# Seven block products in place of eight in the out-projection of a sparse-attention and gated-MLP kernel

## The chip, the cores and the metric

The kernel runs on one core of one Trainium2 chip. The time is the device time of one execution in microseconds (us); the median of three runs of the kernel before is 524.06 us (523.08 to 524.91). The profile is of one execution, whose span from the first to the last instruction is 520.8 us.

## The reference

Eight batches, eight heads, 576 positions, head width 64. Four heads of each batch use a local band of 32 keys, four a strided mask; the attention output x of a batch (576 x 512) feeds a gated block:

```
h = np.maximum(x @ w_in, 0.0)                # 512 -> 1024
u, v = h[..., :512], h[..., 512:]
v_n = (v - mean(v)) / np.sqrt(var(v) + 1e-06)
v_s = np.einsum('ts,bsd->btd', w_spatial, v_n) + b_spatial[None, :, None]
gated = u * v_s
return (gated @ w_out).astype(np.float32)    # 512 -> 512
```

Inputs are float32 (the two weight matrices come as 64-bit words). Every matrix factor is split into a rounded high part and the rest, and each product is the sum of three matmuls: high x high, high x rest, rest x high (PROD, L65).

## The kernel before, in words

**Layout.** A batch's x is held as four tiles (one for two heads, 128 rows of the 512 features), each with a high and a rest part, in the ring x (8 buffers). The positions are 576 = 4 x 128 + 64, for outputs with positions along the columns two halves of 288 (HS, called hf). Rings are sets of buffers that are used in turn: a new tile takes the oldest buffer and waits for all users of the tile that held it.

**Stages of one batch.** *V* (first half of moe_1, L891): four 128 x 512 tiles v = relu(x w_in_v), 12 matmuls of 512 columns each, then a chain on ScalarE, VectorE and GpSimd (relu, batch-norm statistics, normalise, split; chain, L828). *U* (second half of moe_1): eight 128 x 288 tiles u = relu(w_in_u^T x^T), 12 matmuls each, into two buffers of the ring u. *Tail* (moe_tail, L949): the last 64 positions of V, for batches 0 and 1 alone, then for two batches in one. *Gate* (spatial in moe_2, L984): per half, four tiles of 14 matmuls (L997, L1009, L1010), each multiplied into u in place by VectorE (L1019) and then split into high and rest in two buffers of the ring g (L372 or L374, and L382). *Out-projection* (project, L1030): per half, four output tiles e; each sums over four feature blocks f and three products, 12 matmuls of 128 x 288 (L1039), in one bank of the ring m (4 banks of PSUM); then one copy to the ring o (2 buffers, L394 or L396) and one store. moe_2 runs gate half 0, out-projection half 0, gate half 1, out-projection half 1. A batch has 96 matmuls of L1039.

**Order.** All instructions are known ahead and the order of each engine's queue is fixed before the run: a planner (Program.order, L173) walks through a list of operations with modelled costs and, on each engine, takes the ready operation with the smallest key. Keys come from the stage's place in the list plan (L1070), for attention from interpolated due times, and for the setup from the table KEYS. Where an operation may go to several engines (a rounding: ScalarE, VectorE, GpSimd; a rest: VectorE, GpSimd), the planner chooses by its own costs. The entries dp and dpt of KEYS bias that choice up to a given time. The plan is V 0, U 0, tail 0, gate and out-projection 0, the same for batch 1, then V 2, U 2, tail of 2 and 3, gate and out-projection 2, V 3, U 3, and so on. Attention units (32, one for two heads; eight of them before V 1 ends) go between them. The kernel puts idle matmuls (L1172) into gaps of PE early on.

**Weights.** w_in comes in eight tiles (u and v, four each), w_out in four, as 64-bit words: ScalarE (L750), GpSimd or VectorE (L758, L755) and VectorE (L766) turn each into float32, then a rounding and a rest (L382) give the two parts. weights() (L776) sorts the twelve jobs by their keys; the first four use the still empty tile vn as their landing place, then jobs take buffers of the rings g and u in turn (odd jobs g, even jobs u). So the first u tiles of batch 0 take the buffers of the last two even jobs: before, the u weights of block 3 and the w_out rows of block 2.

Of the kernel before, what the change touches and what calls it, by code (L numbers as in the profile page):

```python
# [40 lines left out]
    "a": (-825.9, -1662.1, -696.1, -506.6, 76.7, 35.0, 162.7, 122.5,),  # L41
    "v": (-216.6, -1140.4, -156.0, 19.8,),
    "u": (-158.4, -165.3, 0.3, 367.0,),
    "s": (2476.0, -453.8, 2782.5, 3198.4,),
    "t": (2534.3,),
    "o": (641.4, -137.9, 1268.2, 1486.2,),
    "cst": (-2628.8,),
    "lead": (-0.22,),
    "fill": (170.7, 2011.8, -4312.7, 693.0, -265.9, 735.5,),
    "dp": (844, -15182,),  # L50
    "dpt": (83.09,),
    "lv": (-430.1, -2526.4, -200.5, -140.6,),
    "lu": (-99.7, -488.1, -137.6, -250.6,),
    "lo": (435.1, 82.8, -874.1, 81.6,),
    "ls": (781.6, 39.6, 3113.7, 831.6, 1021.7,),
    "near": (122.22,),
# [6 lines left out]
PROD = ((0, 0), (0, 1), (1, 0))  # L63
FLAT = {2: "p n -> p n", 3: "p a b -> p (a b)", 4: "p a b c -> p (a b c)"}
# [244 lines left out]
def pe_cost(m, n):  # L309
    return max(m / 1.2, 4.8 + 0.4464 * n)  # L310
# [3 lines left out]
def attention_moe(ctx, tc, qT, kT, ks, vl, vs, cst, eye, w_in, w_out, wsp, wtail, out):  # L314
# [14 lines left out]
    w_out_sb = sb.tile([P, 2, NT, DM], F32R, name="w_out_sb")  # L329
# [26 lines left out]
    r_o = Ring(sb, "o", [P, HS], F32, 2)  # L356
# [5 lines left out]
    r_pm = Ring(ps, "m", [P, 512], F32, 4)  # L362
# [86 lines left out]
    def local_attention(t, due, q, kl, v, vin, kin):  # L449
# [45 lines left out]
        for u in range(nu):  # L495
# [22 lines left out]
            def f_e(eng, f0=f0, u=u, m=m):  # L518
# [8 lines left out]
                due - 10, [(ACT, (95 if t in APART else 278) + 0.833 * 2 * STRIDE)], f_e,  # L527
# [200 lines left out]
    def weight(key, fetch, src, n, dst, tok, stage):  # L728
# [7 lines left out]
        if src.dtype == F32:  # L736
            val = lambda: buf().bitcast(F32).rearrange(FLAT[len(buf.ring.shape)])[:, 2 * i * n : 2 * i * n + n]
            load(fetch, val, src, [(buf, i, 0), (buf, i, 1)], P * n * 4)
        else:
# [5 lines left out]
            val = lambda dt=F32: half(1, dt)  # L745
            load(fetch, lambda: raw(I32), src.bitcast(I32), [low, top], P * n * 8)
# [25 lines left out]
        lo_in = [(buf, i, 0), (buf, i, 1)] if src.dtype == F32 else [top]  # L772
        rnd(key, n, lambda: dst(0), val, lo_in, [(*tok, 0)])
        rest(key, n, lambda: dst(1), val, lambda: dst(0), lo_in + [(*tok, 0)], [(*tok, 1)])

    def weights():  # L776
        jobs = []
        for i in range(NT):
            rows = slice(i * P, (i + 1) * P)
            for c, name in enumerate("uv"):  # L780
                cols = slice(c * HF, (c + 1) * HF)
                jobs.append((
# [8 lines left out]
        for n, job in enumerate(jobs):  # L791

            def put(job=job, n=n):
                stage = (first, n) if n < NT else ((r_g if n % 2 else r_u).new(), 0)
                weight(*job, stage)
# [459 lines left out]
```

## Time and profile before

| what | value |
|---|---|
| median of three runs | 524.06 us |
| span of the profiled execution (the page gives no other time of it) | 520.8 us |
| difference between the median and that span | 3.3 us |
| TensorE matmul busy | 508.6 us, 98% |
| VectorE busy | 334.5 us, 64% |
| ScalarE busy | 228.4 us, 44% |
| GpSimd busy | 83.0 us, 16% |
| out-projection matmuls (L1039) | 768, 107.3 us |

The share of an engine is an average over the span; the first 70 us and the rest differ, so the table is to be read together with the stretches below. PE stands for TensorE's matmuls, PEld for its weight loads, DVE for VectorE, ACT for ScalarE, POOL for GpSimd and SP for the queue that issues the DMAs.

### The profile page before, as it was taken

What the parts mean: (1) busy time and instruction counts of PE and PEld (TensorE: products, weight loads), DVE (VectorE), ACT (ScalarE), POOL (GpSimd) and SP (SyncE); (2) the same over time, 40 slices, a digit from 0 to 9 for tenths busy, and PEclk for the clock granted to TensorE, in tenths of its full rate; (3) what the DMA queues carried; (4) which work ended last, traced back from release to release, by engine and by line L of the source; (5) the groups of instructions that cost most, each with busy time, mean ns of one, the idle gap of its engine ahead of it and who ended that gap; (6) DMA issues with size and microseconds to landing.
All of it is one profiled execution on the core that took longest, in us unless ns stands there. A gap on an engine that the chain in (4) does not pass through costs nothing.

```text
span 520.8 us, 14553 instructions
## 1 busy us (share of the span) xinstructions
PE 508.6 (98%) x5980; PEld 467.6 (90%) x5980; DVE 334.5 (64%) x1042; ACT 228.4 (44%) x717; POOL 83.0 (16%) x168
## 2 busy tenths in 40 slices
PE   6899999999999999999999999999999999999997
PEld 3579899889998999989999899998999899998997
DVE  4999996696765758658556667748556553427132
ACT  6778855474533654226432355325432242213111
POOL 2453411133011212002020110102101020001000
PEclk9999999999999999999999999999999999999999
DMA  8968553451333223132233212331102200110011
GB/s 282 338 223 273 186 154 118 135 202 31 102 111 133 79 80 110 47 111 79 80 134 105 85 28 75 133 133 55 49 33 64 87 1 1 47 45 1 1 45 47
DMA packets 26242, 52.65 MB, mean 101 GB/s; under 512 B 3136, under 2 KB 11584, under 8 KB 26176
## 3 DMA queue, kind: packets, MB, share of 16 engines
q1 hardware_dynamic: 26176, 51.72, 29.9%
q8 instruction: 47, 0.77, 0.6%
q14 instruction: 19, 0.16, 0.1%
HBM read 42.27 MB, written 9.44 MB: 99 GB/s over the span
## 4 chain that ended last, share of the span: by engine, by line
PE 87%; DVE 6%; ACT 5%; DMA 1%; issue 1%; SPq 0%; POOL 0%; ACTq 0%; DVEq 0%; POOLq 0%
PE m L1039 20%; PE m L997 19%; PE m L916 17%; PE m L874 17%; PE po L677 3%; PE po L574 3%; PE s L464 2%; PE s L607 2%; PE m L1009 2%; PE m L1010 2%; ACT pl L521 1%; DVE w_in_sb L382 1%; DMA vn<-w_in 1%; ACT ptl L372 1%; DVE x L382 0%
## 5 line engine op out<-in xcount | busy, mean ns | idle before, releaser
L997 PE MATMUL m<-wsp_sb,vn 128*128 128x288 f32 x768 | 111.0, 296 | 0.0
L1039 PE MATMUL m<-g,w_out_sb 128*128 128x288 f32 x768 | 107.3, 298 | 0.0
L916 PE MATMUL m<-x,w_in_sb 128*128 128x288 f32 x768 | 106.2, 297 | 0.5 <-DVE w_in_sb L382 0.5
L997 PEld LDWEIGHTS m<-wsp_sb,vn 128*128 128x128 f32 x768 | 105.2, 189 | 0.9
L916 PEld LDWEIGHTS m<-x,w_in_sb 128*128 128x128 f32 x768 | 103.5, 188 | 2.3 <-DVE w_in_sb L382 0.7
L1039 PEld LDWEIGHTS m<-g,w_out_sb 128*128 128x128 f32 x768 | 103.6, 188 | 0.5
L874 PE MATMUL m<-w_in_sb,x 128*128 128x512 f32 (+1 forms) x408 | 100.2, 399 | 0.5 <-DVE x L382 0.4
L874 PEld LDWEIGHTS m<-w_in_sb,x 128*128 128x128 f32 (+1 forms) x408 | 73.8, 185 | 20.3 <-DVE x L382 1.1
L394 ACT COPY o<-m 128x288 f32<-128x288 f32 x61 | 24.3, 398 | 95.3 <-PE m L1039 80.4
L1019 DVE TENSOR_TENSOR u<-m,u 128x288 f32<-128x288 f32 x64 | 28.0, 452 | 43.5 <-PE m L1010 43.4
L850 POOL TENSOR_TENSOR bn<-bn,sel 128x1 f32<-128x1 f32 (+1 forms) x37 | 21.0, 568 | 185.6 <-DVE bn L845 181.8
L374 POOL TENSOR_SCALAR ptl<-pc 32x64 f32<-32x64 f32 (+3 forms) x74 | 28.8, 389 | 124.2 <-PE po L574 71.7
L521 ACT ACTIVATE pl<-pl,ml 128x64 f32<-128x64 f32 (+1 forms) x140 | 47.0, 338 | 1.8 <-DVE ml L501 1.7
L382 DVE TENSOR_TENSOR x<-po,x 128x288 fp32r<-128x288 f32 x64 | 27.3, 447 | 24.9 <-ACT x L394 24.4
L837 DVE BATCH_NORM_STATS2 bn<-vv 128x6 f32<-128x512 f32 (+1 forms) x37 | 25.4, 689 | 27.5 <-ACT vv L832 27.3
L832 ACT ACTIVATE vv<-m 128x512 f32<-128x512 f32 (+1 forms) x37 | 21.8, 595 | 45.9 <-PE m L874 43.7
L930 ACT ACTIVATE u<-m 128x288 f32<-128x288 f32 x64 | 25.8, 407 | 31.1 <-PE m L916 30.9
L394 ACT CAST x<-po 128x288 fp32r<-128x288 f32 x53 | 20.5, 399 | 39.5 <-PE po L574 27.1
L857 DVE TENSOR_SCALAR vv<-vv,bn 128x512 f32<-128x512 f32 (+1 forms) x37 | 20.5, 555 | 16.3 <-POOL bn L850 16.3
L382 DVE TENSOR_TENSOR g<-u,g 128x288 fp32r<-128x288 f32 x64 | 28.7, 464 | 2.0 <-ACT g L372 0.5
L521 ACT ACTIVATION_READ_ACCUMULATOR pl<-pl,ml 128x1 f32 (+1 forms) x140 | 26.6, 190 | 0.0
L501 DVE CUSTOM_DVE_ANT_0 pl<-s,cst_sb 128x64 f32<-128x64 f32 (+1 forms) x140 | 22.5, 214 | 3.0 <-PE s L464 3.0
(119 smaller groups left out, 564.8 us busy)
## 6 DMA issues: line engine op xcount, KB each, us to landing
q<-qT SPq DMA_DIRECT2D x32, 295.0 KB, 4.3
outT<-o SPq DMA_DIRECT2D x64, 144.0 KB, 1.8
v_raw<-vs SPq DMA_DIRECT2D x15, 512.0 KB, 4.0
v_raw<-vl SPq DMA_DIRECT2D x16, 384.0 KB, 3.6
k<-kT SPq DMA_DIRECT2D x16, 304.0 KB, 4.5
kbd<-ks SPq DMA_DIRECT2D x32, 144.0 KB, 3.6
vn<-w_in SPq DMA_DIRECT2D x4, 512.0 KB, 5.5
u<-w_in SPq DMA_DIRECT2D x3, 512.0 KB, 5.8
```

Of the source, the lines that this page charges most:

```text
L374: eng.tensor_scalar(dst(), src(), 1.0, 0.0, op0=ALU.mult, op1=ALU.add)
L382: eng.tensor_tensor(dst(), src(), f32(hi()), op=ALU.subtract)
L394: eng.copy(dst(), src())
L501: eng.tensor_tensor_reduce(out=p_sb()[:m, u, :], in0=s_ps[u % 2]()[:m, f0 : f0 + 2 * STRIDE], in1=msk[:m], scale=-SCALE, scalar=3.0e38, op ...
L521: eng.activation(p_sb()[:m, u, :], src, AF.Exp, bias=st()[:m, u : u + 1], scale=SCALE if masked else -1.0, **total,)
L837: lambda eng: eng.bn_stats(bn()[:m, 0:6], v()[:m]), [(v,)], [(bn,)],
L874: eng.matmul(v_ps()[:m, :], x_at(kt)[:, a, :], w_in_sb[:, w, kt, HF:], start=(n == 0 and i == 0), stop=(n == NT - 1 and i == 2),)
L916: eng.matmul(u_ps()[:, :HS], w_in_sb[:, w, kt, f * P : (f + 1) * P], xs[NHP * b + kt]()[:, a, r], start=(n == 0 and i == 0), stop=(n == NT ...
L930: lambda eng, u=u, f=f, u_ps=u_ps: eng.activation(u()[:, f * HS : (f + 1) * HS], u_ps()[:, :HS], AF.Relu),
L997: eng.matmul(s_ps()[:, :HS], vn()[:, a, kt, fs], wsp_sb[:, w, kt, r], start=(kt == 0 and i == 0), stop=False,)
L1019: lambda eng, ug=ug, s_ps=s_ps: eng.tensor_tensor(ug(), s_ps()[:, :HS], ug(), op=ALU.mult),
L1039: eng.matmul(o_ps()[:, :HS], w_out_sb[:, w, f, e * P : (e + 1) * P], g[a]()[:, f, :], start=(f == 0 and i == 0), stop=(f == NT - 1 and i = ...
```

## The change

The out-projection of a batch is written as a 2 x 2 by 2 x 2 block product (blocks of features x output columns, and features x position halves) with seven products in place of eight. One product is two feature blocks (r) x two output tiles (j) x three matmuls = 12 matmuls, so a batch has 84. The left factors are four blocks (11, 12, 22 and sums s1 to s4) that are made once from w_out: eight subtractions or additions of 256 columns, and 14 blocks of 256 columns are split where eight 512-column halves were. The right factors are blocks of the gated u or differences of them, made in place in u: eight subtractions of 288 columns for each batch; 14 roundings and 14 rests for each batch where there were eight of each. Sums of products stay in PSUM: two banks (xb) are read after product 11, after s2 and after s3, while more products are added to them; six VectorE additions read a bank and add to a kept part.

Gate and out-projection are stages of their own. V of the next batch stands before the out-projection; the out-projection of batch 0 stands after U and tail of batch 1 (U_FIRST), and u of batch 1 lies in the ring x. The ring o has four buffers. The two banks xb are skipped by other users meanwhile, and the ring m is written as four rings of one bank. The rings g and u keep two buffers; the operands of successive products take the two buffers of g in turn. KEYS is replaced; sorted by the new keys the weight jobs are v2, v0, v1, v3, u2, u0, u1, o1 (two tiles), u3, o0 (two tiles), where "o1" and "o0" are the two halves r of w_out.

```
-    w_out_sb = sb.tile([P, 2, NT, DM], F32R, name="w_out_sb")
+    w_out_sb = sb.tile([P, 2, 2, len(BLOCKS), DM // 2], F32R, name="w_out_sb")
-    r_o = Ring(sb, "o", [P, HS], F32, 2)
+    r_o = Ring(sb, "o", [P, HS], F32, 4)
...
+    def combine(key, n, dst, a, b, op, reads, writes):
+        add(
+            key, [(DVE, 70 + 1.04 * n), (POOL, 120 + 2.3 * n)],
+            lambda eng: eng.tensor_tensor(dst(), a(), b(), op=op), reads, writes,
+            port=(DVE, POOL),
+        )
...
+        combine(key, h, left(sa), right(va), right(vb), ALU.add, [ta, tb, la], [("sum", r, 1)])
+        combine(key, h, right(sa), left(va), right(va), ALU.subtract, [ta, la], [("sum", r, 3)])
+        combine(
+            key, h, left(sb_), left(sa), left(va), ALU.subtract, [ta, ("sum", r, 1), lb], [("sum", r, 2)],
+        )
+        combine(
+            key, h, right(sb_), left(vb), left(sb_), ALU.subtract, [tb, ("sum", r, 2), lb],
+            [("sum", r, 4)],
+        )
+        for name, n, val, reads in (
+            ("11", 1, left(va), [ta]), ("12", 2, vb, [tb]), ("s1", 2, sa, [("sum", r, 1), ("sum", r, 3)]),
+            ("s2", 2, sb_, [("sum", r, 2), ("sum", r, 4)]),
+        ):
+            at = BLOCKS[name]
+            split(
...
+            u = us[b, hf] = (r_x if b in U_IN_X else r_u).new()
...
+    def project_out(b, key):
...
+        def operand(key, r, hf, f, slot):
+            g, half = gs[slot], r
+            at = lambda j: g()[:, 2 * half + j]
+            split(
+                key - KEYS["pre"][0], HS, at, (g, half), block(u[hf], f), [(u[hf], f)],
+            )
+            return at, [(g, half, 0), (g, half, 1)]
...
+        def multiply(key, name, src, bank, slot, first=True):
+            for r in range(2):
+                given = operand(key + 0.74 * r, r, *src[r], slot)
+                for j in range(2):
+                    product(key + 0.74 * r + 0.37 * j, name, r, j, bank[j], given, first)
...
+        multiply(key, "11", [(0, 0), (0, 1)], xb, 0)
+        for r in range(2):
+            total(key, (1, r), (0, r), ALU.subtract, (0, r))
+        multiply(key + step, "s1", [(0, 0), (0, 1)], zb, 1)
+        for j in range(2):
+            keep(key + step, o1[j], xb[j], [(o1[j],)])
+        for r in range(2):
+            total(key + step, (1, 2 + r), (0, r), ALU.subtract, (0, r))
+        multiply(key + 2 * step, "s2", [(0, 0), (0, 1)], xb, 0, False)
+        for r in range(2):
+            total(key + 2 * step, (1, 2 + r), (1, r), ALU.subtract, (1, r))
+        for j in range(2):
+            keep(key + 2 * step, o5[j], zb[j], [(o5[j],)])
+        multiply(key + 3 * step, "s4", [(1, 2), (1, 3)], zb, 1, False)
...
+        multiply(key + 4 * step, "s3", [(1, 0), (1, 1)], xb, 0, False)
+        for j in range(2):
+            join(key + 4 * step, mine(1, 2 + j), zb[j], [(u[1], 2 + j)])
+            store(key + 4 * step, j, 1, mine(1, 2 + j), [(u[1], 2 + j)])
+        for r in range(2):
+            total(key + 4 * step, (0, 2 + r), (0, r), ALU.subtract, (0, r))
+        wb = [r_pm.new() for _ in range(2)]
+        multiply(key + 5 * step, "12", [(0, 2), (0, 3)], wb, 1)
+        for j in range(2):
+            join(key + 5 * step, o5[j], xb[j], [(o5[j],)])
+            store(key + 5 * step, 2 + j, 1, o5[j], [(o5[j],)])
+        multiply(key + 6 * step, "22", [(0, 0), (0, 1)], xb, 0, False)
...
+            join(key + 6 * step, o1[j], wb[j], [(o1[j],)])
+            store(key + 6 * step, j, 0, o1[j], [(o1[j],)])
+        for j in range(2):
+            keep(key + 7 * step, mine(1, j), xb[j], [(u[1], j)])
+            store(key + 7 * step, 2 + j, 0, mine(1, j), [(u[1], j)])
...
+    for b in range(nb):
+        if b and b - 1 not in U_FIRST:
+            plan += [("v", b), ("o", b - 1), ("u", b)]
+        else:
+            plan += [("v", b), ("u", b)]
+        if b < lead:
+            plan.append(("tail", (b,)))
+        elif (b - lead) % 2 == 0:
+            plan.append(("tail", tuple(range(b, min(b + 2, nb)))))
+        if b and b - 1 in U_FIRST:
+            plan.append(("o", b - 1))
+        plan.append(("s", b))
+    plan.append(("o", nb - 1))
```

## Rows read from the trace of the kernel before

**Rows 1.** The page, part 1: busy us (share of span) xinstructions.

```profile
PE 508.6 (98%) x5980; PEld 467.6 (90%) x5980; DVE 334.5 (64%) x1042; ACT 228.4 (44%) x717; POOL 83.0 (16%) x168
```

**Rows 2.** Stretches of the span; the first line names the columns.

```profile
core 0: us, PE busy (x) PEld busy (x) DVE busy (x) ACT busy (x) POOL busy (x), PEclk, DMA share, GB/s
0.00:40.00 40.00, 32.45 (x478) 22.26 (x479) 32.07 (x75) 27.84 (x69) 16.76 (x31) 0.96 0.78 282
40.00:70.00 30.00, 28.69 (x462) 26.09 (x462) 28.71 (x96) 23.92 (x79) 10.06 (x15) 1.00 0.61 202
70.00:190.00 120.00, 120.00 (x1649) 110.50 (x1648) 86.21 (x314) 62.15 (x216) 22.87 (x51) 1.00 0.36 115
...
430.00:521.00 91.00, 87.45 (x633) 84.09 (x631) 32.44 (x78) 17.95 (x40) 3.03 (x6) 1.00 0.08 27
```

**Rows 3.** PE's waits: engine line, releaser, us in total, times, longest.

```profile
PE m L607 <- DMA kbd<-ks: 2.0, 1, 2.0
PE s L464 <- DMA k<-kT: 1.8, 1, 1.8
...
PE m L1009 <- DVE tail L382: 0.8, 1, 0.8
```

**Rows 4.** Groups of PE: line, operation, shapes xcount, busy us, mean ns, idle.

```profile
L1039 PE MATMUL m<-g,w_out_sb 128*128 128x288 f32 x768 | 107.3, 298 | 0.0
...
L1172 PE MATMUL m<-zeros 128*32 128x256 f32 x12 | 5.1, 591 | 0.9 <-DVE zeros L1131 0.9
...
L1172 PE MATMUL po<-zeros 128*32 128x256 f32 x10 | 3.3, 471 | 1.1 <-DVE x L382 1.1
```

**Rows 5.** The chain of waits at the end: start us, us, what.

```profile
497.21 6.40 PE m L1039 x48
...
511.06 6.41 PE m L1039 x48
...
517.53 0.40 ACT o L394
```

**Rows 6.** Groups of VectorE and ScalarE around the out-projection.

```profile
L382 DVE TENSOR_TENSOR g<-u,g 128x288 fp32r<-128x288 f32 x64 | 28.7, 464 | 2.0 <-ACT g L372 0.5
L1019 DVE TENSOR_TENSOR u<-m,u 128x288 f32<-128x288 f32 x64 | 28.0, 452 | 43.5 <-PE m L1010 43.4
...
L394 ACT COPY o<-m 128x288 f32<-128x288 f32 x61 | 24.3, 398 | 95.3 <-PE m L1039 80.4 <-DMA outT<-o 14.4
...
L372 ACT CAST g<-u 128x288 fp32r<-128x288 f32 x28 | 11.2, 432 | 17.0 <-DVE u L1019 17.0
```

**Rows 7.** VectorE in order of time: start us, us, what.

```profile
65.55 1.19 DVE L1019 TENSOR_TENSOR u<-m,u 128x288 f32<-128x288 f32 x3 [0.23 <-PE m L1010]
...
67.13 1.55 DVE L382 TENSOR_TENSOR g<-u,g 128x288 fp32r<-128x288 f32 x4
```

**Rows 8.** Tile w_out_sb: count, duration ns min/median/max, first and last start us.

```profile
L382 DVE TENSOR_TENSOR w_out_sb<-g,w_out_sb x3: 674/677/718, 48.9 to 62.2; 128x512 fp32r<-128x512 f32 x3
...
L382 DVE TENSOR_TENSOR w_out_sb<-u,w_out_sb x1: 693/693/693, 51.4 to 51.4; 128x512 fp32r<-128x512 f32 x1
```

**Rows 9.** ScalarE in order of time, 36 to 54 us: relu of U 0.

```profile
43.69 0.71 ACT L930 ACTIVATE u<-m 128x288 f32<-128x288 f32 x2
...
52.56 0.98 ACT L930 ACTIVATE u<-m 128x288 f32<-128x288 f32 x3
```

**Rows 10.** DMA issues: engine, operation, xcount, KB each, median us to landing.

```profile
outT<-o SPq DMA_DIRECT2D x64, 144.0 KB, 1.8
...
g<-w_out SPq DMA_DIRECT2D x3, 512.0 KB, 6.3
```

**Rows 11.** Stretches from 80 to 100 us, columns as in Rows 2.

```profile
80.00:90.00 10.00, 10.00 (x166) 9.67 (x164) 6.00 (x28) 4.55 (x20) 0.00 (x0) 1.00 0.28 95
90.00:100.00 10.00, 10.00 (x114) 8.46 (x112) 6.40 (x22) 4.58 (x22) 3.00 (x7) 1.00 0.38 131
```

**Rows 12.** The last half out-projection: PE, DVE and ACT in order of time.

```profile
510.90 6.56 PE L1039 MATMUL m<-g,w_out_sb 128*128 128x288 f32 x48
511.17 0.46 DVE L1019 TENSOR_TENSOR u<-m,u 128x288 f32<-128x288 f32 x1 [0.20 <-PE m L1010]
511.66 0.31 DVE L374 TENSOR_SCALAR g<-u 128x288 fp32r<-128x288 f32 x1
512.00 0.46 DVE L382 TENSOR_TENSOR g<-u,g 128x288 fp32r<-128x288 f32 x1
```

More of the change, by code (lines that the diff above doesn't have):

```diff
@@ L361, in attention_moe, with new @@
     r_po = Ring(ps, "po", [P, 512], F32, 2)
-    r_pm = Ring(ps, "m", [P, 512], F32, 4)
+    banks = [Ring(ps, f"m{i}", [P, 512], F32, 1) for i in range(4)]
+    turns = {"n": 0, "held": set()}
+    class r_pm:
+        @staticmethod
+        def new():
+            while turns["n"] % 4 in turns["held"]:
+                turns["n"] += 1
+            turns["n"] += 1
+            return banks[(turns["n"] - 1) % 4].new()
     def rnd(key, n, dst, src, reads, writes, engs=(ACT, DVE, POOL), blocks=False):
@@ L726, in x_tok, with convert @@
         return [(xs[t], i, c0) for i in range(2) for c0 in ((0, 3) if t % NHP < 2 else (0, 1))]
-    def weight(key, fetch, src, n, dst, tok, stage):
+    def convert(key, fetch, src, n, stage):
         buf, i = stage
@@ L745, in weight @@
             val = lambda dt=F32: half(1, dt)
+            spare = lambda: half(0, F32)
             load(fetch, lambda: raw(I32), src.bitcast(I32), [low, top], P * n * 8)
@@ L771, in weight, with split, out_weight @@
             )
-        lo_in = [(buf, i, 0), (buf, i, 1)] if src.dtype == F32 else [top]
-        rnd(key, n, lambda: dst(0), val, lo_in, [(*tok, 0)])
-        rest(key, n, lambda: dst(1), val, lambda: dst(0), lo_in + [(*tok, 0)], [(*tok, 1)])
+        return val, spare, top, low
+    def split(key, n, dst, tok, val, toks):
+        rnd(key, n, lambda: dst(0), val, toks, [(*tok, 0)])
+        rest(key, n, lambda: dst(1), val, lambda: dst(0), toks + [(*tok, 0)], [(*tok, 1)])
+    def combine(key, n, dst, a, b, op, reads, writes):
[4 more added lines that the diff above has]
+        )
+    def out_weight(key, r, parts):
+        h = DM // 2
+        (va, sa, ta, la), (vb, sb_, tb, lb) = parts
+        left, right = (lambda f: lambda: f()[:, :h]), (lambda f: lambda: f()[:, h:])
+        toks = {n: (("sum", r, n),) for n in ("s1", "s2", "s3", "s4")}
+        combine(key, h, left(sa), right(va), right(vb), ALU.add, [ta, tb, la], [("sum", r, 1)])
[13 more added lines that the diff above has]
+            split(
+                key, n * h,
+                lambda j, at=at, n=n: w_out_sb[:, j, r, at : at + n].rearrange("p a b -> p (a b)"),
+                ("w_out", r, name), val, reads,
+            )
     def weights():
@@ L889, in attention_moe, with flat, project_v @@
     vns, tls, us, xtl = {}, {}, {}, {}
-    def moe_1(b, key):
+    def flat(u):
+        return u() if u.ring is r_u else f32(u()).rearrange("p a b -> p (a b)")
+    def project_v(b, key):
         vn = vns[b] = r_vn.new()
@@ L977, in moe_tail, with block, gate @@
             )
-    def moe_2(b, key):
+    def block(u, f):
+        return lambda: flat(u)[:, f * HS : (f + 1) * HS]
+    def gate(b, key):
         vn = vns.pop(b)
         tl, tb = tls.pop(b)
-        gs = {}
+        u = [us[b, hf] for hf in range(2)]
         def spatial(hf, k0):
             r = slice(hf * HS, hf * HS + HS)
-            u = us.pop((b, hf))
-            gh, gl = r_g.new(), r_g.new()
-            gs[hf] = (gh, gl)
             for f in range(NT):
@@ L1162, in attention_moe @@
     for (kind, b), k0 in zip(plan, starts):
-        need = NHP * ((b if kind else b[-1]) + 1)
+        need = NHP * ((b[-1] if kind == "tail" else b) + 1)
         while ahead < need:
@@ L1166, in attention_moe @@
             ahead += 1
[L1167 removed]
+        {"v": project_v, "u": project_u, "tail": moe_tail, "s": gate, "o": project_out}[kind](b, k0)
     ctx.enter_context(tc.manual_schedule())
```

189 lines of the change are left out of this document (105 added, 84 removed).

## The prediction

> **What bounds the kernel now.** I read the engines' totals first: TensorE's matmuls fill 98% of the span, VectorE 64%, ScalarE 44%, GpSimd 16% [rows 1]. An average over the span hides where that holds, so the stretches came next. From 70 to 430 us PE shows no idle time at all; one such stretch is 120.00 busy of 120 [rows 2]. The table of PE's waits has nine entries of at most 2.0 us, all before 66 us [rows 3]. In the first 70 us PE is busy 32.45 + 28.69 = 61.1, so 8.9 us are idle, and the idle matmuls that fill gaps take another 5.1 + 3.3 = 8.4 us [rows 4]; VectorE meanwhile is busy 28.71 of 30 from 40 to 70 us. So there are two kernels here: a start in which VectorE sets the pace and PE loses some 17 us, and from 70 us on a queue of matmuls without a gap. The chain of waits confirms the second part: its last pieces are 48 matmuls of the out-projection back to back, a copy of 0.40 us [rows 5] and the last store. The granted clock is 1.00 in all stretches but the first, 0.96 [rows 2], which is the 2.4 GHz level: a matmul less is worth its full-speed time, and only if its operands come in time.
>
> **The change part by part.**
>
> *Matmuls removed.* The out-projection has 768 matmuls [rows 4]; 48 of them take 6.40 us without a gap [rows 5], 0.1333 us each. (The mean of 298 ns in the group is one instruction's length with its neighbours overlapped, not its cost.) Twelve fewer in each of eight batches: 96 x 0.1333 = 12.8 us. All of it lies on the path, since PE has no idle time after 70 us. That is the whole gain; the rest of this part is what may be given back.
>
> *Work added in each stage.* For a batch VectorE, ScalarE and GpSimd get six roundings (0.432 us on ScalarE), six rests (0.464 on VectorE), eight subtractions (as the rests: two tiles of 288 columns from SBUF) and six joins (a bank plus a tile, as the gate's multiply, 0.452) [rows 6]. The eight copies out of PSUM stay. If ScalarE rounds, VectorE gets 20 operations more. By length that is 20 x 0.46 = 9.2 us a batch; but VectorE starts them closer together: four rests in a row took 1.55 us, 0.39 each, three multiplies 1.19 us, 0.40 each [rows 7]. So 7.8 to 9.2 us a batch. From 70 to 190 us VectorE has 120 - 86.2 = 33.8 us free [rows 2], and two out-projections need 18.4 of them at most. Over the span there is room.
>
> *Inside a stage it is closer.* A stage has 84 matmuls, 84 x 0.1333 = 11.2 us, and 14 rests + 8 subtractions + 6 joins = 28 VectorE operations: 28 x 0.39 = 10.9 us at the close spacing, 28 x 0.46 = 12.9 us by length. Six of them (the rests of products 11 and s1, and two subtractions) can be done before the stage, while V of the next batch runs, because both buffers of g are then free. That leaves 22: 8.6 to 10.1 us of 11.2. Attention matmuls that fall into the stage give VectorE more time, but bring work of their own.
>
> *Waits added.* Each product's operand takes the place of the operand of two products before; behind its last matmul of one half r come 18 others, 2.4 us, before PE needs the new one. The chain is a rounding (0.31 on VectorE or 0.43 on ScalarE), a rest of 0.46 and the hand-overs between engines. On VectorE alone a rounding and a rest follow one another with 0.03 us between them (511.66 + 0.31 = 511.97, then 512.00 [rows 12]); between engines I allow 0.2 each time, the 0.20 us that VectorE waited for PE before the multiply there. So about 0.2 + 0.43 + 0.2 + 0.46 + 0.2 = 1.5 us of 2.4, with 0.9 us to spare for whatever stands ahead in VectorE's queue; a transpose or a normalisation there is about as long. Queued behind a late product on PE is everything, since PE takes its queue in order. I bound a stage's stall between 0 and 12.9 - 11.2 = 1.7 us and take 0.2 for each of seven stages, nearest to the row of close starts: 1.4 us. The last stage has no other PE work beside it, yet VectorE is nearly free there (32.44 of 91 us busy [rows 2]): 0 to 1.7, I take 0.5.
>
> The Trainium skill, "VectorE: DVE Perf Modes", section "The TRN2 errata", gives a float32 tensor_tensor (N + 151) / 0.96 ns, which for N = 288 is an estimate of 457 ns. Rows 6 agree on the length, rows 7 do not agree on the spacing; by the page a stage would need 28 x 0.457 = 12.8 us on VectorE.
>
> *PSUM.* The two banks xb are read three times amid the sum; each copy or join (0.40 or 0.45 us) has another product's 1.6 us of PE before the bank is written again. This costs nothing unless the reader is late, which is the same stall as above. u(b+1) waits for stores out of u, which land in 1.8 us [rows 10]; its first half uses the other buffer, 6.4 us of PE, which hides it. The larger ring o removes waits of ScalarE's copies for stores (they are in its 95 us of idle time [rows 6]), which PE never felt.
>
> *The start.* w_out's preparation grows: eight combinations at about 0.40 us (256 columns; the 288-column operation takes 0.46), and rests of six 512-column and two 256-column pieces in place of four of 512: 6 x 0.68 + 2 x 0.40 - 4 x 0.68 = 2.2 us [rows 8]. So 5.4 us more on an engine that is full until 70 us. Worse is where it stands: buffers. By the new order of jobs the first u tiles of batch 0 take the buffers of one o1 tile and one o0 tile, and the second o0 tile can be loaded only when o1's sums are finished, with 6.3 us of landing time [rows 10]. Before, the second half's relus began at 52.56 [rows 9], right behind the one w_out rest at 51.4 to 52.1 that held their buffer [rows 8]; the other w_out rests went on to 62.2 and held nobody. Now all of them come first. PE has only four banks to run ahead. The best case is that the preparation is moved ahead of attention of batch 1 and no time is lost, and the wait for the tail (0.8 us [rows 3]) goes: -1. The worst is that it ends as late as before plus its growth: 62.9 + 5.4 = 68.3, 16 us behind 52.1, less the attention matmuls that can fill the hole (some 4 us of them lie between 55 and 67 us): +12. For the middle: a first o1 tile ready at 49.6 (as before), 6.3 landing, about 4.5 of conversion and sums ends at 60.4, 8 us late, of which 4 are filled: +4.
>
> The order gives and takes here too. Out-projection 0 stood between 68 and 93 us and was PE's work while VectorE finished attention of batch 1; now V 1 follows gate 0 and wants that attention some 13 us earlier. But the splits for it go too, and VectorE had 4.0 + 3.6 = 7.6 us free from 80 to 100 us [rows 11]. I take this as even; it is inside the -1 to +12.
>
> *The end.* As before, a copy and a store follow the last matmul; two stores come 0.4 us apart: +0.2.
>
> *Sum.* -12.8 + 4 + 1.4 + 0.5 + 0.2 = -6.7. The profiled execution's span of 520.8 becomes 514.1; the 3.3 us by which the median of the runs exceeds that span stay: **517.4 us**.
>
> **The rivals.**
>
> *The start costs nothing and no stage stalls.* For it: VectorE's 33.8 free us after 70, and the 0.9 us to spare in each operand's chain. Against: the chain of buffers. 520.8 - 12.8 + 0.2 + 3.3 = 511.5.
>
> *U 0 waits for w_out's sums in full.* The start costs 11: 520.8 - 12.8 + 11 + 2.1 + 3.3 = 524.4, no change. For it: of the twelve weight jobs o0 has the largest key and o1 the third largest, so VectorE does attention that is ready before them. Against: what it does meanwhile is attention of batch 1, which is wanted soon after.
>
> *VectorE paces every out-projection, and the kernel is slower.* If each operation costs its length, and none is done ahead because VectorE is busy with V's chain and attention when V of the next batch runs, a stage takes 12.9 us in place of 11.2: 8 x 1.7 = 13.6 us, more than the matmuls saved: 520.8 - 12.8 + 13.6 + 4 + 0.2 + 3.3 = 529.1. It decides from the point at which VectorE needs more than 11.2 us within a stage; the kernel is then slower from about 12.3 us on. Against: rows 7. The page's formula above, taken as spacing, would make it so.
>
> **How the numbers follow.** Forecast (512.5 to 521.5) 0.48; the better rival (below 512.5) 0.25; the start in full 0.14; VectorE paces 0.10; else 0.03. Range 509.5 to 525: it takes in the first three and leaves out the slower rival and some of the tails. No change is within 0.3% of 524.06, 522.5 to 525.6, about what a measurement can tell. Faster: 0.48 + 0.25 + 0.03 of the third = 0.76. Same: 0.08 of the third and 0.01 else = 0.09. Slower: 0.10 + 0.03 + 0.02 = 0.15.
>
> **What would show it.** The groups of out-projection matmuls: 672, in runs of 12 of 1.60 us. PE's waits after 100 us: under 2 us in all if the stages hold, one of 0.2 to 1.7 us in every stage on a rest of g if VectorE paces. PE's idle time and idle matmuls before 80 us, 17 us now: 21 by the forecast, with a hole near 50 to 60 us behind a relu of u that waits for w_out; 28 or more by the second rival. VectorE's total rises to about 400 us. The forecast is wrong if PE's idle time in the stages exceeds 4 us, or if the start loses nothing.

## The result, and the profile after

The changed kernel takes 517.02 us (median of 4 runs, 516.58 to 517.66), the kernel before, run beside it, 523.98 (523.08 to 524.91). The ratio is 0.9874, 95% interval 0.9855 to 0.9892: faster by 1.3%. The profiled run took 516.93 us with a span of 515.1, against 520.8 before: 5.7 us less. That pair shows less than the medians do (523.98 - 517.02 = 7.0 us): runs of the kernel before take 1.8 to 2.2 us more than their spans (524.06 us had a span of 522.0, 522.79 one of 520.8), so the profiled execution lies some 1.3 us under the median. The accounts by stretches below explain 5.7 us; where a run at the median loses the other 1.3 no trace here shows.

The engines' totals, columns as in [rows 1]:

```profile
PE 498.4 (97%) x5890; PEld 456.0 (89%) x5890; DVE 363.6 (71%) x1123; ACT 269.5 (52%) x823; POOL 104.3 (20%) x205
```

TensorE lost 10.2 us of work [rows 1]; VectorE gained 29.1, ScalarE 41.1, GpSimd 21.3. The same in stretches, to be laid beside [rows 2]:

```profile
core 0: us, PE busy (x) PEld busy (x) DVE busy (x) ACT busy (x) POOL busy (x), PEclk, DMA share, GB/s
0.00:40.00 40.00, 29.07 (x455) 19.98 (x456) 29.59 (x65) 30.22 (x73) 19.26 (x35) 0.87 0.76 266
40.00:70.00 30.00, 28.64 (x370) 25.58 (x369) 27.77 (x83) 21.53 (x58) 9.96 (x17) 1.00 0.64 216
70.00:190.00 120.00, 119.68 (x1778) 108.64 (x1777) 96.46 (x353) 81.59 (x290) 32.51 (x68) 1.00 0.40 126
190.00:430.00 240.00, 240.00 (x2733) 224.10 (x2732) 164.05 (x513) 113.89 (x355) 38.33 (x79) 1.00 0.24 75
```

The picture has kept its two parts. From 70 us on PE still has no gap worth naming (0.32 us of 120, 0 of 240). Before 70 us it is busy for 57.7 us where it was 61.1: 3.4 us more of idle time, and the granted clock of the first 40 us fell from 0.96 to 0.87. PE's waits [rows 3], by line, releaser, us in total, times, longest:

```profile
PE m L620 <- DMA kbd<-ks: 5.3, 2, 3.8
...
PE m L981 <- ACT vv L892: 0.8, 1, 0.8
PE m L981 <- DVE w_in_sb L395: 0.5, 1, 0.5
PE m L1112 <- DVE u L1135: 0.4, 1, 0.4
```

Only the last of these is in an out-projection (L1112). The groups of PE [rows 4]:

```profile
L1112 PE MATMUL m<-g,w_out_sb 128*128 128x288 f32 x672 | 91.9, 296 | 0.4 <-DVE u L1135 0.4
...
L1308 PE MATMUL m<-zeros 128*32 128x256 f32 x20 | 6.1, 466 | 0.9 <-DVE zeros L1267 0.9
...
L1308 PE MATMUL po<-zeros 128*32 128x256 f32 x8 | 3.1, 531 | 2.5 <-DVE x L395 2.5
```

96 of 768 matmuls are gone, as planned, and the idle matmuls grew from 8.4 to 9.2 us. Where the loss lies shows when both traces are laid one over the other at the first matmul of U 0. PE ahead of it, changed kernel:

```profile
33.60 1.66 PE L690 MATMUL po<-pts,xt 128*64 128x72 f32 x32 [0.32 <-POOL pts L387]
35.19 8.66 PE L934 MATMUL m<-w_in_sb,x 128*128 128x512 f32 x36
43.69 1.76 PE L981 MATMUL m<-x,w_in_sb 128*128 128x288 f32 x12
```

and the kernel before:

```profile
30.93 1.22 PE L677 MATMUL po<-pts,v_raw 128*64 128x72 f32 x32 [0.54 <-POOL pts L374]
32.08 6.32 PE L874 MATMUL m<-w_in_sb,x 128*128 128x512 f32 x24
38.23 0.96 PE L916 MATMUL m<-x,w_in_sb 128*128 128x288 f32 x6
```

U 0 starts 43.69 - 38.23 = 5.5 us later. From there to the end the kernel takes 515.1 - 43.7 = 471.4 us in place of 520.8 - 38.2 = 482.6, 11.2 less: the 12.8 us of matmuls, less 1.6. So, in this pair of executions, -11.2 + 5.5 = -5.7, and the start's part of it is over before U 0 begins: the last attention unit of batch 0 comes 2.7 us later, and 36 matmuls of V 0 stand behind it in place of 24.

### The profile page after: what moved, and what is told of

Read it like the earlier page. It is cut to its first block, busy times and chain, and to the rows that moved or that the text cites. A ratio compares the mean times of both kernels' runs of the same rounds, so it can differ in the third digit from the quotient of the medians.

```text
span 515.1 us, 14660 instructions
## 1 busy us (share of the span) xinstructions
PE 498.4 (97%) x5890; PEld 456.0 (89%) x5890; DVE 363.6 (71%) x1123; ACT 269.5 (52%) x823; POOL 104.3 (20%) x205
## 4 chain that ended last, share of the span: by engine, by line
PE 81%; DVE 9%; ACT 3%; DMA 2%; POOL 2%; issue 1%; SPq 1%; POOLq 0%; ACTq 0%; DVEq 0%
PE m L1062 20%; PE m L981 18%; PE m L1112 15%; PE m L934 15%; PE po L690 3%; PE po L587 3%; PE s L477 2%; PE m L1074 2%; PE m L1075 2%; PE s L620 2%; DVE bn L897 1%; DMA k<-kT 1%; DMA kbd<-ks 1%; DVE vn L395 1%; DVE vv L917 1%
## 5 line engine op out<-in xcount | busy, mean ns | idle before, releaser
L1112 PE MATMUL m<-g,w_out_sb 128*128 128x288 f32 x672 | 91.9, 296 | 0.4 <-DVE u L1135 0.4
L1112 PEld LDWEIGHTS m<-g,w_out_sb 128*128 128x128 f32 x672 | 89.8, 188 | 2.1 <-issue 0.6
L387 POOL TENSOR_SCALAR ptl<-pc 32x64 f32<-32x64 f32 (+3 forms) x91 | 34.7, 381 | 125.4 <-PE po L587 71.6
L910 POOL TENSOR_TENSOR bn<-bn,sel 128x1 f32<-128x1 f32 (+1 forms) x37 | 24.0, 649 | 155.9 <-DVE bn L905 152.4
L385 ACT CAST g<-u 128x288 fp32r<-128x288 f32 x77 | 33.2, 435 | 41.0 <-PE m L1112 23.5
L1084 DVE TENSOR_TENSOR u<-m,u 128x288 f32<-128x288 f32 x56 | 24.6, 452 | 37.2 <-PE m L1075 36.6
L407 ACT CAST x<-po 128x288 fp32r<-128x288 f32 x60 | 23.5, 399 | 42.9 <-PE po L587 23.2
L395 DVE TENSOR_TENSOR g<-u,g 128x288 fp32r<-128x288 f32 x96 | 43.3, 463 | 2.5 <-ACT g L385 1.7
L995 ACT ACTIVATE u<-m 128x288 f32<-128x288 f32 x56 | 22.6, 407 | 35.6 <-PE m L981 35.6
L385 ACT COPY ptl<-pc 32x320 f32<-32x320 f32 (+3 forms) x79 | 28.0, 354 | 3.3 <-DVE pc L558 1.8
```

The source lines that it names most:

```text
L385: eng.copy(dst(), src())
L387: eng.tensor_scalar(dst(), src(), 1.0, 0.0, op0=ALU.mult, op1=ALU.add)
L395: eng.tensor_tensor(dst(), src(), f32(hi()), op=ALU.subtract)
L910: lambda eng: eng.tensor_tensor(bn()[:m, 9:10], bn()[:m, 8:9], sel[:m, 0:1], op=ALU.pow),
L1084: lambda eng, ug=ug, s_ps=s_ps: eng.tensor_tensor(ug(), s_ps()[:, :HS], ug(), op=ALU.mult),
L1112: eng.matmul(o_ps()[:, :HS], w_out_sb[:, w, r, BLOCKS[name], j * P : (j + 1) * P], at(a), start=(first and r == 0 and i == 0), stop=(r == ...
```

## The experiments

My theory after the comparison: the start's loss is made ahead of U 0 by the new order, and the stages cost nearly nothing. The rivals: U 0 is held by w_out's sums and buffers, as predicted; the added work costs the start as much in any order; VectorE or V's place sets the stages. (The letters are those of each expectation.) Where "order kept" is said, each engine's queue is that of the changed kernel but for the edit named; otherwise the planner orders anew.

**1. Eight products in the new order** (planned anew). The out-projection goes back to eight block products with plain rows of w_out and four operand buffers; V ahead and the new keys stay. From the edit:

```
-                        out_weight(key, i, [parts[i, 0], parts[i, 1]])
+                    split(
+                        key, DM, lambda j: w_out_sb[:, j, f], ("w_out", f), val,
...
-        multiply(key, "11", [(0, 0), (0, 1)], xb, 0)
...
+            for e in range(NT):
+                o_ps = r_pm.new()
+                for f in range(NT):
```

> The changed kernel with eight products in place of seven: w_out kept as before (eight 512-column splits, no sums), 96 matmuls a batch, eight roundings and eight rests a batch, four operand buffers; the new order, the new keys and V ahead of the out-projection stay (the planner orders it anew). Theory A (the matmuls are the whole gain, the stages cost PE nothing): 517.0 + 12.8, less up to 3 us for the lighter start: 527 to 530 us, so the order alone makes the kernel before slower by 3 to 6. Rival B (the new order brings the gain and the seven products pay for their own additions): 515 to 522. Rival C (the stages of the seven products lose several us in waits): 523 to 526.

Measured: 542.87 us, ratio 1.0369 [1.0345, 1.0393]; far above what any theory gave. The edit moved the planned order, and PE stands idle where neither kernel does:

```profile
70.00:100.00 30.00, 26.07 (x554) 21.42 (x556) 20.12 (x98) 14.78 (x64) 3.68 (x9) 1.00 0.47 143
100.00:130.00 30.00, 24.25 (x550) 21.10 (x537) 23.59 (x98) 23.46 (x90) 9.41 (x25) 0.77 0.48 141
```

As a comparison of whole times it is a miss. Its end can still be used, since there all kernels have the same work left: from the first matmul of U 6 to the end it takes 541.6 - 441.7 = 99.9 us, the kernel before 520.8 - 420.8 = 100.0, the changed one 515.1 - 417.6 = 97.5. So over these last 100 us the order by itself is worth nothing, and seven products save 2.4 us in two out-projections, where 3.2 were removed.

**2. V behind the out-projection** (planned anew). `plan += [("o", b - 1), ("v", b), ("u", b)]` in place of `[("v", b), ("o", b - 1), ("u", b)]`.

> The changed kernel with V of the next batch behind the out-projection for batches 2 to 7, so that each out-projection follows its gate directly, as the last one does already. Theory A (operands are made in time even without V's cover, as in the last stage, where PE does not wait): 516 to 518.5 us. Rival B (V's 11 us are what lets the first operands be made ahead; without them each of six stages waits 0.5 to 1.7 us): 520 to 527, with PE idle time in every stage.

Measured: 517.94 us, ratio 0.9899 [0.987, 0.9929]. By the medians V's place ahead is worth 0.9 us, and the intervals overlap. No wait of PE for an operand of an out-projection is among its waits of 0.2 us and more: the stages don't live on the head start that V gives VectorE.

**3. More VectorE work in every stage** (order kept). Each subtraction is followed on its engine by one of half its width into a scratch tile, 64 in all. VectorE's busy time grew from 363.6 to 381.4 us, by 17.8 or 2.2 a stage, where the expectation had 1.8:

```
+  eng.tensor_tensor(extra_sb, at_x()[:, : HS // 2], at_dst()[:, : HS // 2], op=op)
```

> The changed kernel with the planner's order kept as it is; each of the eight subtractions of a batch is followed on its engine by one more of half its width into a scratch tile that nobody reads: some 0.2 us each, 1.8 us a stage. Theory A (VectorE is at its limit within the stages, 94 to 98% busy there, though 71% over the span): PE waits 0.5 to 1.4 us a stage, 521 to 528 us. Rival B (VectorE has room, a stage moves its other work behind): 516.5 to 518.5.

Measured: 520.92 us, ratio 0.9946 [0.9929, 0.9962]; between the theories. 2.4 us of the loss stand before U 0 (46.1), where the edit adds nothing. The last attention unit of batch 0 starts 0.5 us later (34.10), and it and the 36 matmuls of V 0 behind it take 2.19 and 9.99 us where they took 1.66 and 8.66. From 30 to 35 us PE was busy for 2.69 us (3.87 in the changed kernel), and from 35 to 40 us the granted clock was 0.58 (1.00 there); why the start ran so is open. From U 0 on it is 519.4 - 46.1 = 473.3 against 471.4: 1.9 us for 17.8 of work. PE's waits in the out-projection grew to

```profile
PE m L1113 <- DVE u L1136: 0.8, 1, 0.8
PE m L1113 <- DVE g L396: 0.5, 2, 0.3
PE m L1113 <- DVE o L410: 0.2, 1, 0.2
```

So VectorE isn't what paces a stage now. Of the work added, 15.9 us cost PE nothing, about 2 us a stage (an estimate, 15.9 / 8), and at this load the first operands come late. What still more work would cost wasn't tried.

**4. One load of w_in behind the keys** (order kept otherwise). `issued.insert(loads[15], issued.pop(loads[12]))` puts the second load of w_in behind the keys of the second strided unit.

> The changed kernel with the planner's order kept on every engine but for one transfer: the second load of w_in (512 KB), issued at 10.4 us between the keys of the first two strided units, is issued behind the second keys. Theory A (the start lost its time because these keys land late, PE waits 5.3 us for them in place of 2.0): PE's waits for them fall to 2 to 3 us and 513.5 to 515.5 us. Rival B (VectorE sets the start's pace, what is gained at the keys is lost behind them): the waits fall, but 516.5 to 517.5.

Measured: 517.79 us, ratio 0.9892 [0.987, 0.9914]. The waits for keys fell from 5.3 to 3.2 us, and U 0 started later, at 45.6. The keys aren't what holds it. What took their place is instructive: GpSimd stood longer at its step on that load, and the values behind it came at 20.62 in place of 18.72.

**5. No sums of w_out** (order kept). The eight sums are left out, and the blocks that should hold s1 and s2 take plain rows of w_out:

```
-            lambda eng: eng.tensor_tensor(dst(), a(), b(), op=op), reads, writes,
+            lambda eng: n == HS and eng.tensor_tensor(dst(), a(), b(), op=op), reads, writes,
...
+            ("11", 1, left(va), [ta]), ("12", 2, vb, [tb]), ("s1", 2, va, [("sum", r, 1), ("sum", r, 3)]),
+            ("s2", 2, vb, [("sum", r, 2), ("sum", r, 4)]),
```

> The order of the changed kernel is kept instruction by instruction; the eight sums of w_out blocks (about 0.40 us each, 3.2 us of VectorE and GpSimd) are left out, and the blocks that should hold s1 and s2 take plain rows of w_out, so the products are wrong and the matmuls the same. Theory A (the start's loss sits before the first matmul of U 0, and the sums, which VectorE does after about 36 us, hold nobody there): the first U matmul stays at 43.7 +- 0.4 us, the waits of 1.3 us inside U 0 shrink, 515.5 to 517.0. Rival B (U 0 waits for the sums of w_out, as the prediction had it): the first half of the 4 us comes back, 512.5 to 514.5.

Measured: 516.31 us, ratio 0.9845 [0.9823, 0.9868], not to be told from the changed kernel (0.9855 to 0.9892). U 0 started at 44.1, and the waits inside it stayed (0.6 and 0.8 us). The late relus of U 0 started at 59.27 us (59.21 with the sums), both times right behind a cast of w_out on ScalarE, and PE didn't wait for them. In this order nobody waits for the sums, and the wait that the prediction put a price on costs nothing.

**6. Other buffers for w_out's tiles** (planned anew). `(r_g if name == "o" else r_u).new()` keeps w_out's second tiles out of the buffers of u.

> The second tile of each w_out job takes a buffer of ring g as the first does, so that no tile of U 0 waits for a sum or a split of w_out; the order is planned anew from the same keys. Theory A (U 0 is late because attention and V of batch 0 end late, whoever holds its buffers): the first U matmul comes at 41 to 46 us, as the new order happens to fall, and the time stays at 515 to 520. Rival B (the buffers hold U 0): the relus of its second half come 2 us or more earlier against the first matmul of U 0 than now (59.2 after 43.7), PE's waits there go, 512 to 514.5.

Measured: 530.8 us, ratio 1.0124 [1.0101, 1.0148]; outside both. The new order starts U 0 at 46.7 and loses 5.9 us of PE from 100 to 130 us, far behind the edit, so it says nothing about the buffers.

**7. The start's old keys** (planned anew). The keys of attention, loads, weights, V, U and S are those of the kernel before.

> The changed kernel with the keys of the kernel before for attention, loads, weights, V, U and S (those of the out-projection and of its preparation stay); the order is planned anew. Theory A (the start's +5.5 us is the new order's doing: the last attention unit of batch 0 stands later and 12 matmuls of V 0 stand behind it in place of ahead): the first U matmul comes at 38 to 40.5 us, as before (38.2), and the whole takes 511.5 to 514.5. Rival C (the added preparation of w_out costs the start as much in any order): the first U matmul or the second half of U 0 is as late as now, 516 to 519.

Measured: 528.22 us, ratio 1.0094 [1.0072, 1.0116]; slower than the kernel before. U 0 starts at 41.2, but the matmuls of its second half stand still. VectorE, ScalarE and PE of this kernel in order of time:

```profile
51.77 1.34 PE L477 MATMUL s<-k,q 64*32 64x64 f32 x72 [2.69 <-issue]
...
55.75 0.68 DVE L395 TENSOR_TENSOR w_out_sb<-u,w_out_sb 128x512 fp32r<-128x512 f32 x1
...
56.55 1.32 ACT L995 ACTIVATE u<-m 128x288 f32<-128x288 f32 x4 [0.27 <-DVE w_out_sb L395]
...
57.01 9.14 PE L981 MATMUL m<-x,w_in_sb 128*128 128x288 f32 x48 [3.89 <-ACT u L995]
```

The four relus of the first half wait for the split of a w_out tile that lies in a buffer of u (it ends at 56.43), and PE for the relus, 3.9 us. Just before, PE had stood 2.7 us ahead of 72 scores with no releaser in the profile ("issue"); without that stop it would have come to the wait for the relus earlier. Behind the wait 48 matmuls take 9.14 us, against 6.4 at full speed: from 55 to 60 us, in which PE was busy for 2.99 us, the granted clock was 0.50 (1.2 GHz). This is the prediction's mechanism, in the order that the old keys make. The changed kernel's keys avoid it.

**8. The same without the sums** (order of 7 kept, edit of 5).

> The kernel with the start's old keys (528.2 us; in it PE waits 3.9 us, once, for a relu of U 0 that comes behind a split of w_out at 56.4), its order kept, with the eight sums of w_out blocks left out as before (3.3 us of VectorE; the products are wrong). Theory G (the mechanism that the prediction named is real in that order: buffers of u are held until w_out is summed and split): the wait of 3.9 us shrinks to between 0.5 and 2.5 us, 524 to 526.5. Rival H (loads and splits of w_out hold the buffers, the sums add nothing): the wait stays above 3 us, 527.5 to 528.5.

Measured: 526.32 us, ratio 1.0049 [1.0026, 1.0072], 0.4% under 7. PE's wait hardly changed:

```profile
PE m L981 <- ACT u L995: 3.7, 1, 3.7
```

By the wait theory H has it: the splits and what stands ahead of them in the queues hold the buffer, not the sums. The time lies in G's range, but the 1.9 us between the medians don't show in the two profiled runs (spans 524.4 and 526.3), so this pair settles the wait and no more.

**9. Twelve matmuls of V 0 ahead of the last unit** (PE's order alone changed).

```
+        fillers.pop(issued[last][1], None)
...
+        issued[last:last] = up
```

> The changed kernel with PE's order alone altered: the four operations of V 0 on the second feature block (12 matmuls) stand before the last strided unit of batch 0, not behind it, and the 6 idle matmuls that stood there are left out; all other engines keep their order. Theory A (12 matmuls of V 0 behind that unit are part of the start's loss, and PE stood idle there for lack of work): the first U matmul comes at 42 to 42.8 us, 515 to 516. Rival D (the operands of those matmuls, splits of w_in that end at about 32.4, come no earlier than the unit's, 33.6): the unit is pushed back by as much as V gains, the first U matmul stays at 43.7 +- 0.4, 516.5 to 517.5.

Measured: 522.56 us, ratio 0.9973 [0.9959, 0.9987]; wrong by both theories. PE:

```profile
34.08 0.80 PE L959 MATMUL m<-w_in_sb,x 128*128 128x512 f32 x1 [4.75 <-ACT w_in_sb L410]
35.28 5.06 PE L959 MATMUL m<-w_in_sb,x 128*128 128x512 f32 x11 [0.41 <-DVE w_in_sb L420]
40.27 1.44 PE L715 MATMUL po<-pts,xt 128*64 128x72 f32 x32
```

Their weights are there at 35.3, after the unit's operands (33.6), so the unit now waits for V. From 30 to 35 us PE was busy for 0.80 us, the idle matmuls being left out, and from 35 to 40 us the granted clock was 0.50 (1.2 GHz): 11 matmuls took 5.06 us, 0.46 each, against 0.24 in the changed kernel. The changed order is right to put them last, given that w_in comes so late. That moves the question to why it does.

**Why w_in comes late.** GpSimd, PE and SP of the changed kernel in order of time, other engines left out:

```profile
16.07 0.64 POOL L776 TENSOR_SCALAR vn<-vn 128x512 int32<-128x512 uint8 x1 [10.99 <-DMA vn<-w_in]
...
16.80 1.68 POOL L387 TENSOR_SCALAR ptl<-pc 32x320 f32<-32x320 f32 x4
...
17.60 1.19 PE L620 MATMUL m<-kbd,q 128*32 128x36 f32 x64 [1.57 <-DMA kbd<-ks]
...
18.72 2.19 PE L587 MATMUL po<-ptl,v_raw 128*64 128x96 f32 x24
...
20.95 0.33 SPq L414 DMA_DIRECT2D v_raw<-vs  x1
...
21.32 0.91 SPq L414 DMA_DIRECT2D vn<-w_in  x2
...
22.27 1.01 SPq L414 DMA_DIRECT2D g<-w_in  x1
```

and of the kernel before:

```profile
15.20 2.17 POOL L374 TENSOR_SCALAR ptl<-pc 32x320 f32<-32x320 f32 x5 [8.99 <-DVE pc L545]
...
16.82 1.21 PE L574 MATMUL po<-ptl,v_raw 128*64 128x96 f32 x24
...
18.07 0.33 SPq L401 DMA_DIRECT2D v_raw<-vs  x1
...
18.44 0.43 SPq L401 DMA_DIRECT2D u<-w_in  x1
```

Read it upwards. Three loads of w_in go out from 21.3 on because SP's queue stands at the load of v_raw, whose buffer is free when the first unit's values are done, at 20.9 (18.0 before). The values are late for three reasons: GpSimd stands at a step on w_in that waits for its DMA, with four copies (ptl) behind it; PE takes the second unit's scores first, and those wait for their keys until 17.60; and the values then take 2.19 in place of 1.21 us, at a granted clock of 0.50 from 15 to 20 us. The last three experiments take these apart.

**10. The local order of before, with idle matmuls** (GpSimd's step behind the copies, PE's values ahead of the second scores, 12 and 3 idle matmuls).

> The changed kernel's order, but for two places from 14 to 21 us put back as in the kernel before: GpSimd does its four copies of the first local unit ahead of the step on w_in (which waits for a DMA), and PE does that unit's values ahead of the second strided unit's scores; 12 idle matmuls stand before the first scores and 3 before the values. Theory A (the start's +5.5 us begins here: values that end at 20.91 in place of 18.03 hold the buffer of one load, and three loads of w_in stand behind it in SP's queue): the values start at about 17.1 us in place of 18.72, the loads of w_in at 21.3 and 22.3 go out at 18.5 to 19.5, the first U matmul comes at 40.5 to 42 us, 513 to 515.2. Rival F (VectorE, busy 94 to 100% from 25 to 40 us, sets U 0 whatever the loads do): the loads are earlier but the first U matmul stays at 43.2 to 44, 516.2 to 517.5.

**11. Idle matmuls alone** (order kept; `warm(bank, (12, 5)[waits.index(n)])` ahead of the two scores).

> The changed kernel with its order kept; 12 and 5 idle matmuls are added where PE waits for the keys of the first two strided units, so that PE doesn't stand idle from 11.1 to 14.8 and from 16.0 to 17.6 us. Both theories: the granted clock of 15 to 20 us rises from 0.50 to 0.9 or more and the 24 matmuls on the values at 18.72 take 1.2 us in place of 2.19. Rival E (the half clock there is what the start lost): the first U matmul at 41.5 to 42.5 us, 514.3 to 515.7. Theory A (it is the order of GpSimd and PE, and the half clock costs what the values take longer): at 42.6 to 43.6, 516.0 to 517.

Measured: 10 takes 520.1 us, ratio 0.9922 [0.9897, 0.9947]; 11 takes 517.69, 0.9874 [0.9845, 0.9903]. The clock stayed at 1.00 from 5 to 20 us in both, but a new stop came. PE of 11, profiled run (519.77 us), and its instruction queue from 20 to 23 us:

```profile
19.86 0.88 PE L593 MATMUL po<-ptl,v_raw 128*64 128x96 f32 x16
23.24 0.91 PE L593 MATMUL po<-ptl,v_raw 128*64 128x96 f32 x8 [2.50 <-issue]
```

```profile
q8 instruction: 1, 0.02, 2.0%
```

"issue" means that PE waited for nothing that the profile shows. Experiment 10 has such a stop of 2.16 us, in the scores at 19.96. Both come after the same number of matmuls (178 and 177 in the timeline since the second local unit's scores), with a transfer of the instruction queue just before. That PE ran out of instructions, having been given more of them to run early, isn't shown: the changed kernel has such a transfer between 19 and 22 us and no stop, and experiments 1, 7 and 8, whose edits add no idle matmuls, have stops of the same kind (1.6 and 2.1, 2.7 and 1.6, 2.7 and 2.1 us, all in scores). So 10 and 11 don't tell A from its rivals by their times. In 10 the loads of w_in did go out from 19.71 on, 1.6 us before those of the changed kernel, and U 0 still came at 46.8, 3.1 later: early loads alone, with that stop behind them, don't bring it forward. The other three runs of 11 took 517.1 to 518.2 us at a clock of 1.00, the changed kernel 516.6 to 517.7: the idle matmuls bought nothing there; whether the stop is in them no trace shows.

**12. The cause taken away, with 6 idle matmuls** (the load of 4 behind the keys, GpSimd's step behind the copies; PE's order kept).

```
+        issued.remove(low)
...
+        issued.insert(max(i for i, x in enumerate(issued) if x[1] in parts) + 1, low)
...
+        issued.insert(loads[15], issued.pop(loads[12]))
```

> The changed kernel's order, but for the cause as the traces so far have it: the second load of w_in goes behind the keys of the first two strided units, GpSimd's step on that load (which stood waiting for the DMA with four copies of the first local unit behind it) goes behind those copies, and 6 idle matmuls stand where PE waits for the first keys. In three kernels of the same order the first U matmul follows the end of that unit's values by 22.8 us (20.91 and 43.69 in the changed kernel, 22.81 and 45.6 with the later load alone, 24.15 and 47.0 with 17 idle matmuls). Theory A (values, and the loads behind the buffer that they free, carry U 0): scores end at 18.0 us, values at 19.2 to 20.2, the first U matmul comes at 42.0 to 43.0, 515.0 to 516.4. Rival F (VectorE's queue, full from 25 us, carries U 0): the values are earlier, the first U matmul stays at 43.4 to 44, 516.6 to 517.4. If PE stalls once more for its own instructions: 518 or more.

Measured: 516.45 us, ratio 0.9881 [0.9864, 0.9899]; span 513.8. Its GpSimd, PE and SP:

```profile
15.51 1.68 POOL L400 TENSOR_SCALAR ptl<-pc 32x320 f32<-32x320 f32 x4 [10.46 <-DVE pc L571]
...
17.43 1.21 PE L600 MATMUL po<-ptl,v_raw 128*64 128x96 f32 x24 [0.51 <-ACT ptl L398]
...
19.05 0.92 SPq L427 DMA_DIRECT2D vn<-w_in  x2
...
32.71 1.22 PE L703 MATMUL po<-pts,xt 128*64 128x72 f32 x32 [1.31 <-POOL pts L400]
...
42.88 1.74 PE L994 MATMUL m<-x,w_in_sb 128*128 128x288 f32 x12
```

The values end 2.3 us earlier, at 18.6, the loads go out 2.3 earlier; U 0 starts 0.8 earlier. This agrees with a chain from the values to U 0, as 4 does in the other direction (values at 22.8, U 0 at 45.6); 11 does too (24.2 and 47.0), but there a stop of PE itself held both. In this direction 1.5 of 2.3 us are lost again: the last unit waits 1.3 us for GpSimd's copies, where it waited 0.3. And 0.8 us is little beside the 2.4 by which U 0 moved in experiment 3 with no edit ahead of it. This version and the changed kernel can't be told apart by their times (intervals 0.9864 to 0.9899 and 0.9855 to 0.9892), so the repair isn't shown to be worth anything.

## Why the prediction was right, and where it wasn't

*Matmuls: -12.8.* Right. A stage of 84 runs without a gap in 11.1 us (227.39 to 238.47), 12.8 before. Of the 12.8 us for all batches 11.2 are left behind the start of U 0, in the profiled pair.

*Stages: +1.4, and +0.5 for the last.* Too much. The waits in the out-projections are 0.4 us in all, and PE loses 0.3 more from 70 to 190. VectorE is as full inside a stage as the step said, and fuller:

```profile
227.40:238.40 11.00, 11.00 (x85) 11.00 (x84) 10.38 (x33) 8.14 (x32) 1.65 (x3) 1.00 0.33 114
285.90:299.20 13.30, 13.30 (x188) 12.88 (x187) 12.99 (x56) 10.51 (x44) 3.02 (x6) 1.00 0.44 137
...
500.20:511.20 11.00, 11.00 (x86) 10.98 (x84) 9.54 (x25) 4.95 (x13) 0.00 (x0) 1.00 0.19 66
```

87 to 98% busy with PE at 100%: the operands come just in time. That closeness, which the step put a price on, cost next to nothing until experiment 3 added work. Two subtractions of the last stage show the spacing:

```profile
501.00 0.46 DVE L799 TENSOR_TENSOR u<-u,u 128x288 f32<-128x288 f32 x1
501.37 0.45 DVE L799 TENSOR_TENSOR u<-u 128x288 f32<-128x288 f32 x1
```

They are 0.46 us long and start 0.37 apart. The Trainium skill ("VectorE: DVE Perf Modes", section "The TRN2 errata") gives a formula that makes 457 ns for one, an estimate, and by it 28 would take 12.8 us. The length agrees, the spacing doesn't, as [rows 7] said; the two stages above with nothing but out-projection on PE took 11.1 and 11.2 us.

The forecast of VectorE's total, 400 us, was wrong by 36: it counted 20 operations more a batch on VectorE, 160, while VectorE got 1123 - 1042 = 81 instructions more, ScalarE 106 and GpSimd 37 [rows 1]. The planner spread the work; that is the term that was mis-sized.

*The start: +4.* The size was near, but by luck: the place was wrong. Idle time and idle matmuls before 70 us are 12.3 + 9.2 = 21.5 us, 21 by the forecast; but the "hole near 50 to 60 us behind a relu of u" isn't there. The relus of U 0's second half did move from 52.56 [rows 9] to the group at 59.21 (L995), behind the last split of w_out out of a buffer of u (58.44 to 59.13), not far from the 60.4 of the step. PE of the changed kernel, and that group:

```profile
58.21 1.49 PE L620 MATMUL s<-kbd,q 128*32 128x36 f32 x128
59.67 1.87 PE L981 MATMUL m<-x,w_in_sb 128*128 128x288 f32 x12
```

```profile
59.21 1.01 ACT L995 ACTIVATE u<-m 128x288 f32<-128x288 f32 x3
```

PE had done 84 of the 96 matmuls of U 0, filled the time with 128 scores and took up the last 12 without a wait. V 0 itself had ended 5.5 us later, so U 0 was late anyway; inside U 0 PE lost 0.5 and 0.8 us, for a split of w_in and a relu of V 0. What failed in the step "Worse is where it stands: buffers" is its price, a wait of PE of 8 us with 4 of them filled. Experiments 5 and 7 show both sides: with this order the sums hold nobody, with the old keys the wait is there, 3.9 us, and the kernel is slower than before. What stands in its place is a loss ahead of U 0, and a chain from 14 to 23 us that is part of it: a GpSimd step that waits for a DMA, values, a buffer, three loads. In experiments 4 and 12 U 0 moves with the values, by 1.9 us for 1.9 and by 0.8 for 2.3; that it moves through the loads isn't shown (in 10 they went out earlier and U 0 came later), and that the chain explains all 5.5 us isn't either. In experiment 12 4.7 us remain, and whether VectorE's fuller queue from 25 to 40 us or the order of its work makes them stays open.

*The end: +0.2.* From the last matmul's end to the span's it grew from 3.3 to 3.7 us: near.

*Around the span: +3.3.* Not what it seemed. It is 517.0 - 515.1 = 1.9 for the changed kernel and 1.8 to 2.2 for the kernel before in its runs beside the experiments; the rest of the 3.3, some 1.3 us, is how far the profiled execution lies under the median. The step added that difference back, which is right for a forecast from median to median: -6.7 by the sum, -7.0 measured. Against the one profiled span the forecast of 514.1 is 1.0 us too low, and the 1.4 us too much around it hide that. The nearness of 0.4 us is in part luck.

The first rival (no cost at the start) is out by the 5.5 us, the second (the sums in full) by experiment 5, the third (VectorE paces) by PE's waits of 0.4 us in all out-projections and by experiment 3: 17.8 us more of VectorE's work cost PE 1.9.

## What to carry to other kernels

Where TensorE is gapless, matmuls taken away are worth most of their time (11.2 of 12.8 us here), and extra work on an engine that is 87 to 98% busy inside a stage can still cost almost nothing (0.4 us here, with two operand buffers in turn); measure how much room there is by adding a known amount. Before the gapless part, count the order of every in-order queue: a step on GpSimd that waits for a DMA holds the copies behind it, and through a buffer the loads behind them. An edit that makes a planner order anew changes more than the edit (experiment 1 is 19 us slower than the kernel it partly goes back to); keep the order and change one thing.

## What the runs showed of the hardware

PE can stop for 1.6 to 2.7 us with nothing that the profile names as a cause. In experiments 10 and 11 the stop came after the same number of matmuls, beside a transfer of the instruction queue; experiments 1, 7 and 8 have such stops too, and what they wait for stays open.

What half clock costs depends on what stands behind it. From 15 to 20 us the changed kernel runs at a granted clock of 0.50 (1.2 GHz), after PE had been busy for 1.1 us of the 5 before; experiment 12 runs at 1.00 over its first 40 us and starts U 0 only 0.8 us earlier, with two other repairs in it. In experiment 3 the low clock stands right ahead of U 0 (0.58 from 35 to 40 us), and the last unit and V 0's matmuls took 1.9 us longer, of the 2.4 by which U 0 came later.

Banks of PSUM can be read in the middle of a sum at little cost: eight of a batch's 14 reads are such, and PE's waits in all out-projections are 0.4 us.
